# Row sums as a matrix product with ones stationary, rows divided before their turn, and key chunks taken three at a time in a BigBird attention kernel

## The chip, the core and the metric

The kernel runs on one core of one Trainium2 chip. Its time is the device time of one execution in microseconds (us), the median of three runs. Beside the runs there is one execution that was recorded by the hardware profiler; all durations below come from that one. TensorE is PE in the rows, its weight loads are PEld, VectorE is DVE, ScalarE is ACT, GpSimd is POOL, and SP is the queue from which most DMAs are issued.

## What is computed

Block-sparse attention over 4 batches, 8 heads, 768 positions and a head width of 64, and behind it a mixture of experts in which every token goes to one of 8 experts:

```python
scores = np.matmul(q, k.transpose(0, 1, 3, 2)) / np.sqrt(64)
scores = np.where(mask, scores, -1e9)          # window, first and last block, 3 sampled blocks a row
attn = np.exp(scores - scores.max(-1, keepdims=True))
attn = attn / (attn.sum(-1, keepdims=True) + 1e-09)
x = rows of np.matmul(attn, v)                 # (3072, 512): heads side by side
logits = x @ w_gate                            # (3072, 8); the largest chooses the expert
y = np.maximum(x[e's rows] @ w1[e], 0) @ w2[e] # 512 -> 1024 -> 512
out = softmax(logits)[chosen] * y
```

All of it is in 32-bit floats; the mask alone enters as bf16.

## The kernel before

**Attention.** The 32 heads are worked off as 16 pairs (4 batches by 4 pairs, number n in the code), each in two halves of 384 queries: 32 halves. Positions are spread so that a tile of 128 partitions holds six chunks of 128 keys. For each pair `load` (L88) brings k, q and v, and `turn` (L189) turns k and q on TensorE, so that the head width lies on partitions: three transposes into one PSUM bank, a copy of 384 columns to SBUF by VectorE, three more transposes into the same bank, and a copy by ScalarE. The k of the next pair is turned in the first half of this one, and its q in the second.

For each chunk of 128 keys `scores` (L208) does, for the two heads of the pair, the product of keys and queries (L216; the heads lie on partitions 0 to 63 and 64 to 127) and adds the mask as a second product (L219). ScalarE takes the exponential of both heads in one instruction (L221), and VectorE adds it up over the chunks into `esum` (L227), so that the sum over keys is left as a sum over partitions. `attend` (L229) multiplies with v: v's 64 columns of a head are stationary, the 384 columns of `e` move, and the two heads write partitions 0 to 63 and 64 to 127 of one bank `op` (L236). After the sixth chunk ScalarE copies `op` to `oT` (L241): outputs with the head width on partitions and queries along columns, not yet divided.

`rows_out` (L244) makes rows of them. First come the sums: for each of three query chunks and two heads a matmul in which 128 columns of `esum` are stationary and one column of ones moves (L252). Then three matmuls take `oT` as stationary and a matrix `mix` as moving operand (L257): `mix` is an identity with the gate's weights beside it, for each head apart, 144 columns, so that one product gives the turned rows and both heads' shares of the gate's logits. VectorE adds 1e-9 to the sums, takes their reciprocals (six columns), multiplies rows and logit shares by them while it copies them out of PSUM (L260 to L280), and SP stores the rows to `x_rows` in HBM. After the fourth pair of a batch `gate` takes the softmax over the experts.

**The order of work.** TensorE's and GpSimd's orders are those of the program text; VectorE's, ScalarE's and SP's come from a scheduler. The loop at L668 goes over steps of `GR = 2` chunks, three steps a half: it issues the scores of step i, and then the products with v of step i - 1. In the middle step of a half stand `turn` and, between its two sets of transposes, `rows_out` of the half before. PSUM has eight banks: two tiles of two banks for scores (`ps_s`), two banks for `op` (`ps_o`), one for turns (`ps_t`), one for `rows_out` and the routing (`ps_x`). Six `e` tiles are held.

**Routing.** When three of the four batches are done, `ranks`, `count`, `layout_a` and `tokens` (at pairs 12 to 14) work out on VectorE, with a few small matmuls, which tokens make the first 5 tiles of 128 rows of one expert each. So SP can load weights and GpSimd can gather rows before attention ends. The rest of the tokens are laid out in the same way behind it.

**Experts.** 28 such tiles follow, each with 4 MB of weights (two loads of 2 MB from SP), 32 matmuls in `layer1` (L622) and 8 wide ones in `layer2` (L642). `rows_out` of the very last half stands inside the first tile's `layer1`.

A matmul of 32-bit floats is one instruction in the program and two in the trace.

## Time and profile before

| | us |
|---|---|
| median of three runs | 846.18 (846.07 to 846.46) |
| the profiled execution | 846.65 |
| its span, first to last instruction | 844.9 |
| TensorE busy in the span | 820.4 |
| VectorE busy | 293.4 |
| ScalarE busy | 214.6 |
| GpSimd busy | 69.3 |
| attention, to the last product with v | about 421.9 |
| experts, from there | about 423.0 |

The first rows of the profile's page give busy time by engine. Busy time of TensorE says little by itself, because matmuls overlap and each is recorded from its start to its end: what one costs in a stream is the distance from its start to the start of the next. So the timeline is the view that prices TensorE's work here: it merges equal instructions that follow each other into one row and gives the start of each row to a hundredth of a microsecond. For VectorE and ScalarE the duration of an instruction is close to its price. "Granted clock" is the share of TensorE's full clock (2.4 GHz) that it was given in a stretch.

### The profile page before, as it was taken

Reading aid. Unit: us, or ns where it says so; the run is one execution under the profiler, and the core shown is the slowest. Engines: PE = TensorE matmul, PEld = TensorE weight load, DVE = VectorE, ACT = ScalarE, POOL = GpSimd, SP = SyncE. Lnnn points to the kernel's source line nnn. Section 1 sums busy time; section 2 is a strip of 40 time slices with the busy share of each in tenths; the row PEclk is TensorE's granted clock in tenths of the full one; section 3 lists DMA queues with packets and bytes.
Section 4 is the critical chain, followed back from the end, with each engine's and each line's share of the span. In section 5 each row is a group of like instructions: output and inputs, shape, how many; then the busy total and the mean of one; then the engine's idle time right before and its main releaser. Section 6 shows DMA issues by size and latency. Waiting matters only on the chain.

```text
span 844.9 us, 12494 instructions
## 1 busy us (share of the span) xinstructions
PE 820.4 (97%) x5104; PEld 519.8 (62%) x5104; DVE 293.4 (35%) x613; ACT 214.6 (25%) x306; POOL 69.3 (8%) x102
## 2 busy tenths in 40 slices
PE   7999999999999999899999999999999999999993
PEld 4555455455455455454587767686867777776681
DVE  5454565554554555854533001110101011111110
ACT  2444444544544544444411100000000000000000
POOL 4000000000000000002002111010101010111000
PEclk9999999999999999999999999999999999999997
DMA  7122221222321222842048989989899999999930
GB/s 168 41 74 57 75 67 47 60 73 57 76 70 44 62 71 58 277 178 70 20 164 299 331 326 325 334 304 337 305 335 309 336 312 336 325 332 340 324 127 10
DMA packets 119238, 157.52 MB, mean 186 GB/s; under 512 B 56435, under 2 KB 72819, under 8 KB 119156
## 3 DMA queue, kind: packets, MB, share of 16 engines
q1 hardware_dynamic: 112544, 142.32, 51.7%
q0 software_dynamic: 4480, 13.75, 4.2%
q8 instruction: 44, 0.72, 0.4%
q10 hardware_dynamic: 2132, 0.41, 0.2%
q14 instruction: 38, 0.31, 0.1%
HBM read 143.79 MB, written 13.73 MB: 186 GB/s over the span
## 4 chain that ended last, share of the span: by engine, by line
issue 44%; PE 42%; DMA 5%; POOL 4%; DVE 3%; another core or an unknown queue 0%; POOLq 0%; ACT 0%; DVEq 0%
PE s L216 15%; PE op L236 14%; DMA out_dram<-zo,sB 5%; PE xr L252 4%; PE s L219 3%; POOL xg L597 3%; PE xr L257 3%; PE tp L197 3%; POOL out_dram L654 1%; DVE esum L227 1%; PE first L197 0%; DVE allow L151 0%; DVE orA L561 0%; DVE kT L201 0%
## 5 line engine op out<-in xcount | busy, mean ns | idle before, releaser
L630 PEld LDWEIGHTS hp<-xgT,w 128*128 128x128 f32 x1792 | 206.3, 192 | 12.6 <-issue 12.6
L630 PE MATMUL hp<-xgT,w 128*128 128x128 f32 x1792 | 209.1, 275 | 0.0
L645 PE MATMUL zp<-w,hT 128*128 128x512 f32 x448 | 197.0, 593 | 0.9 <-DVE hT L635 0.9
L221 ACT ACTIVATE e<-s 128x768 f32<-128x768 f32 x192 | 155.6, 812 | 94.6 <-PE s L219 92.2
L216 PE MATMUL s<-qT,kT 64*128 64x384 f32 x768 | 167.4, 514 | 0.0
L227 DVE TENSOR_TENSOR esum<-esum,e 128x768 f32<-128x768 f32 x128 | 122.6, 958 | 69.5 <-ACT e L221 62.9
L236 PE MATMUL op<-e,v_sb 128*64 128x384 f32 x768 | 144.8, 499 | 0.0
L645 PEld LDWEIGHTS zp<-w,hT 128*128 128x128 f32 x448 | 83.1, 190 | 95.3 <-issue 94.2
L637 ACT ACTIVATE hT<-hp 128x512 f32<-128x512 f32 x33 | 19.7, 597 | 340.7 <-PE hp L630 337.8
L216 PEld LDWEIGHTS s<-qT,kT 64*128 64x128 f32 x768 | 64.0, 188 | 64.8 <-ACT e L221 37.4
L236 PEld LDWEIGHTS op<-e,v_sb 128*64 128x64 f32 x768 | 46.7, 136 | 80.1 <-issue 79.9
L653 DVE TENSOR_SCALAR zo<-zp,xg 128x512 f32<-128x512 f32 x23 | 17.3, 751 | 213.0 <-PE zp L645 194.0
L219 PE MATMUL s<-pen,oh 64*128 64x384 bf16 x384 | 63.6, 325 | 0.0
L227 DVE TENSOR_TENSOR esum<-e 128x768 f32<-128x768 f32 x32 | 30.7, 958 | 65.3 <-ACT e L221 65.3
L635 DVE TENSOR_SCALAR hT<-hp 128x512 f32<-128x512 f32 x23 | 15.9, 691 | 95.9 <-PE hp L630 95.9
L252 PEld LDWEIGHTS xr<-ones,esum 128*128 128x128 f32 x384 | 45.4, 192 | 1.2 <-DVE esum L227 1.2
L654 POOL DMA_INDIRECT out_dram<-zo,sB x23 | 23.3, 1014 | 269.6 <-DVE zo L653 269.6
L252 PE MATMUL xr<-ones,esum 128*128 128x1 f32 x384 | 44.9, 244 | 0.0
L219 PEld LDWEIGHTS <-oh 64*128 64x128 bf16 x384 | 19.5, 95 | 25.3 <-issue 0.9
L257 PE MATMUL xr<-mix,oT 128*128 128x144 f32 x192 | 31.4, 300 | 0.0
L597 POOL DMA_INDIRECT xg<-x_rows,gA x5 | 6.7, 1336 | 245.2 <-PE s L219 243.9
L257 PEld LDWEIGHTS xr<-mix,oT 128*128 128x128 f32 x192 | 25.4, 191 | 0.0
(185 smaller groups left out, 299.1 us busy)
## 6 DMA issues: line engine op xcount, KB each, us to landing
w<-in_moe_w_dram SPq DMA_DIRECT2D x56, 2048.0 KB, 9.7
k_sb<-in_k_dram SPq DMA_DIRECT2D x32, 192.0 KB, 3.4
v_sb<-in_v_dram SPq DMA_DIRECT2D x16, 384.0 KB, 3.1
x_rows<-xb SPq DMA_DIRECT2D x16, 384.0 KB, 3.8
q_sb<-in_q_dram SPq DMA_DIRECT2D x30, 192.0 KB, 3.2
q_sb<-in_q_dram ACTq DMA_DIRECT2D x2, 192.0 KB, 6.1
xg<-x_rows,gB POOLq DMA_INDIRECT x23, 7.7
out_dram<-zo,sB POOLq DMA_INDIRECT x23, 8.0
```

Source lines behind the costliest of these rows:

```text
L197: nc.tensor.transpose(tp[:, c * P : (c + 1) * P], src[:, half * HC + c].rearrange("p h d -> p (h d)"), ident[:],)
L216: nc.tensor.matmul(s[:, hh, :CW], lhsT=kT[r, c * P : (c + 1) * P], rhs=qT[r, cols], start=True, stop=False)
L219: nc.tensor.matmul(s[:, hh, :CW], lhsT=oh[r, c, :], rhs=pen[r, cols], start=False, stop=True)
L221: nc.scalar.activation(e[:], s[:, :, :CW], AF.Exp, scale=scale)
L227: nc.vector.tensor_add(t[:], es[(n, half, 0)][:] if c == 1 else t[:], e[:])
L236: nc.tensor.matmul(op[hh * D : (hh + 1) * D, :], lhsT=v_sb[:, hh, c, :], rhs=e[:, hh, :], start=(c == 0), stop=(c == NCH - 1),)
L252: nc.tensor.matmul(xr[:, HC * M + 2 * m + hh : HC * M + 2 * m + hh + 1], lhsT=esum[:, hh, m * P : (m + 1) * P], rhs=ones[:], start=True, s ...
L257: nc.tensor.matmul(xr[:, m * M : (m + 1) * M], lhsT=oT[:, m * P : (m + 1) * P], rhs=mix[:, pr, :], start=True, stop=True)
L597: nc.gpsimd.indirect_dma_start(out=xg[:], out_offset=None, in_=x_d[: N - S, :] if i < KA else x_d[:, :], in_offset=bass.IndirectOffsetOnAx ...
L630: nc.tensor.matmul(hp[:, m, :], lhsT=st[i]["w1"][:, c, fb * P : (fb + 1) * P], rhs=st[i]["xT"][:, c, :], start=(c == 0), stop=(c == DB - 1),)
L645: nc.tensor.matmul(zp[:], lhsT=st[i]["hT"][:, fb, :], rhs=st[i]["w2"][:, fb, :], start=(fb == 0), stop=(fb == FB - 1),)
L654: ins = nc.gpsimd.indirect_dma_start(out=out[:, :], out_offset=bass.IndirectOffsetOnAxis(ap=of("s", i, P), axis=0), in_=zo[:], in_offset=N ...
```

## The change

- `ones` becomes 64 columns wide. A new function `divide` runs once a half, straight behind the last products with v: the 64 columns of ones are stationary, `esum` moves (384 columns, for each head), and the two heads write partitions 0 to 63 and 64 to 127 of one bank `sp`. Every one of 64 partitions then holds the head's sums. ScalarE copies them to `ss` and adds 1e-9, SP stores one row a head into `sums` by a DMA from SBUF to SBUF, and VectorE takes reciprocals of `ss` in three instructions of 128 columns and multiplies `oT` with them.
- `rows_out` has no sums, reciprocals or multiplications left: three matmuls with `mix`, which needs only one set of gate columns now (136 columns), a copy of the rows and a copy or an addition of the logits, by VectorE. It runs for the pair before (n - 1), not for the half before. `oT` has four buffers.
- `GR` is 3: two steps a half. Eight `e` tiles are held.
- `turn` takes a `ps_s` tile (two banks): six transposes in a row, then two copies, both by ScalarE.
- PSUM: three tiles of two banks in `ps_s`, one bank for `op`, one in `ps_x`, which `divide` and `rows_out` share. `layer2` has its banks in a pool of its own.
- Routing of the first 5 tiles starts a half later, because rows come out later. At the end of attention `rows_out` of the last two halves stand in the middle of the first `layer1` and behind it.
- `judge`, a check of ranges that runs off the path in the second stage, reads the new shape of `sums`.

```diff
-    ps_t = ctx.enter_context(tc.tile_pool(name="ps_t", bufs=1, space=PSUM))
-    ps_o = ctx.enter_context(tc.tile_pool(name="ps_o", bufs=2, space=PSUM))
+    ps_o = ctx.enter_context(tc.tile_pool(name="ps_o", bufs=1, space=PSUM))
...
-    lend(lent, ps_s=2)
+    lend(lent, ps_s=3)
...
-    def turn(b, pr, which, first=None):
+    def turn(b, pr, which):
...
+        tp = upper["ps_s"].tile([P, 2, 512], F32, name="tp", tag="s")
+        for c in range(NCH):
+            nc.tensor.transpose(
+                tp[:, c // HC, c % HC * P : (c % HC + 1) * P], src[:, c].rearrange("p h d -> p (h d)"), ident[:],
+            )
         for half in range(2):
...
+            nc.scalar.copy(dst[:, half * CW : (half + 1) * CW], tp[:, half, :CW])
...
+    def divide(n, half):
+
+        oT, esum = ops_[(n, half)], esums.pop((n, half))
+        sp = ps_x.tile([P, CW], F32, name="sp", tag="xr")
+        for hh in range(2):
+            nc.tensor.matmul(sp[hh * D : (hh + 1) * D, :], lhsT=ones[:], rhs=esum[:, hh, :], start=True, stop=True)
+        ss = work.tile([P, CW], F32, name="ss")
+        nc.scalar.activation(ss[:], sp[:], AF.Copy, bias=1e-9)
+        row = 2 * (2 * n + half)
+        nc.sync.dma_start(sums[row : row + 2, :], ss.rearrange("(h d) q -> h d q", h=2)[:, 0, :])
+        r = work.tile([P, CW], F32, name="r")
+        for m in range(HC):
+            nc.vector.reciprocal(r[:, m * P : (m + 1) * P], ss[:, m * P : (m + 1) * P])
+        nc.vector.tensor_mul(oT[:], oT[:], r[:])
...
     def rows_out(n, half):
...
-        M = P + 2 * E
-        xr = ps_x.tile([P, HC * M + 2 * HC], F32, name="xr")
+        M = P + E
+        xr = ps_x.tile([P, HC, M], F32, name="xr")
         for m in range(HC):
-            for hh in range(2):
-                nc.tensor.matmul(
-                    xr[:, HC * M + 2 * m + hh : HC * M + 2 * m + hh + 1], lhsT=esum[:, hh, m * P : (m + 1) * P], rhs=ones[:],
-                    start=True, stop=True,
-                )
...
+            nc.tensor.matmul(xr[:, m, :], lhsT=oT[:, m * P : (m + 1) * P], rhs=mix[:, pr, :], start=True, stop=True)
...
+        nc.vector.tensor_copy(xb[:, half * HC : (half + 1) * HC, :], xr[:, :, :P])
...
+            nc.vector.tensor_copy(sofar, xr[:, :, P:])
         else:
...
+            nc.vector.tensor_add(sofar, sofar, xr[:, :, P:])
...
-    GR = 2
-    steps = [(n, half, g) for n in range(len(pairs)) for half in range(2) for g in range(NCH // GR)]
+    GR = NCH // 2
+    steps = [(n, half, g) for n in range(len(pairs)) for half in range(2) for g in range(2)]
...
                 attend(n, half, c)
+            if g == 1:
+                divide(n, half)
...
-            turning = turn(*pairs[n + 1], half) if n + 1 < len(pairs) else iter(())
-            next(turning, None)
-            if i > 3:
-                rows_out(*steps[i - 2][:2])
-            for _ in turning:
-                pass
-
-            if (n, half) == (NA, 0):
+            if n + 1 < len(pairs):
+                turn(*pairs[n + 1], half)
+            if n > 0:
+                rows_out(n - 1, half)
+
+            if (n, half) == (NA, 1):
                 ranks("A", 0, TA)
-            if (n, half) == (NA, 1):
+            if (n, half) == (NA + 1, 0):
                 count("A")
                 layout_a()
...
-    layer1(0, lambda: rows_out(*steps[-1][:2]), lambda: turn_x(1))
+    layer1(0, lambda: rows_out(len(pairs) - 1, 0), lambda: turn_x(1))
+    rows_out(len(pairs) - 1, 1)
```

What the diff does to the orders stands below at three places. In the rows of an order an instruction is named with its line, what it writes and reads, and the shape that it writes; a matmul of 32-bit floats is one instruction there.

TensorE before, at the middle step of a half (`op` the products with v, `tp` a turn, `xr` sums with ones and then rows with `mix`, `s` scores):

```order
L236 MATMUL op<-e,v_sb 64x384 x4
L197 MATMUL tp<-ident,q_sb 128x128 x3
L252 MATMUL xr<-ones,esum 128x1 x6
L257 MATMUL xr<-mix,oT 128x144 x3
L197 MATMUL tp<-ident,q_sb 128x128 x3
L216 MATMUL s<-qT,kT 128x384 x2
```

TensorE now, from the last scores of a half's first step (`sp` is the new sums):

```order
L215 MATMUL s<-pen,oh 128x384
L232 MATMUL op<-e,v_sb 64x384 x6
L245 MATMUL sp<-esum,ones 64x384 x2
L212 MATMUL s<-qT,kT 128x384 x2
L215 LDWEIGHTS oh
```

and from the last scores of its second step:

```order
L215 MATMUL s<-pen,oh 128x384
L232 MATMUL op<-e,v_sb 64x384 x6
L196 MATMUL tp<-ident,k_sb 128x128 x6
L262 MATMUL xr<-mix,oT 128x136 x3
L212 MATMUL s<-qT,kT 128x384 x2
```

Six matmuls that write one column each have given way to two that write 384, which follow products of their own shape; a half goes from scores to products with v twice, where it went three times.

VectorE before, over one half in the steady stretch:

```order
L227 TENSOR_TENSOR esum<-e 128x768
L227 TENSOR_TENSOR esum<-esum,e 128x768 x2
L201 COPY kT<-tp 128x384
L260 TENSOR_SCALAR sums<-xr 128x6
L261 RECIPROCAL r<-sums 128x6
L267 TENSOR_TENSOR xb<-xr,r 128x3x64 x2
L272 TENSOR_TENSOR lg<-xr,r 128x48
L279 TENSOR_TENSOR lgn<-lgn,lg 128x24
L280 TENSOR_TENSOR lgn<-lgn,lg 128x24
L227 TENSOR_TENSOR esum<-esum,e 128x768 x2
```

VectorE now:

```order
L223 TENSOR_TENSOR esum<-e 128x768
L223 TENSOR_TENSOR esum<-esum,e 128x768
L252 RECIPROCAL r<-ss 128x128 x3
L223 TENSOR_TENSOR esum<-esum,e 128x768
L253 TENSOR_TENSOR oT<-oT,r 128x384
L223 TENSOR_TENSOR esum<-esum,e 128x768 x2
L266 COPY xb<-xr 128x384
L271 TENSOR_TENSOR lgn<-lgn,xr 128x24
```

The turn's copy and the small instructions are gone; three reciprocals of 128 columns and a multiplication of 384 stand among the additions of `esum`.

SP now, where the first experts' weights are loaded (`xeA` the expert of a tile, `w_0` and `w_1` its weights):

```order
L249 DMA sums<-ss 2x384
L590 TENSOR_LOAD xeA
L590 ISA x2
L593 ISA
L593 DMA w_0_177<-in_moe_w_dram 128x4x1024
L249 DMA sums<-ss 2x384
L590 TENSOR_LOAD xeA
L590 ISA x2
L596 ISA
L596 DMA w_0_179<-in_moe_w_dram 128x8x512
```

The small stores of the sums, one a half, stand between these loads; before there was no such store.

## Rows read from the trace of the kernel before

**Rows 1.** The page, part 1: busy us and share of the span.
```profile
PE 820.4 (97%) x5104; PEld 519.8 (62%) x5104; DVE 293.4 (35%) x613; ACT 214.6 (25%) x306; POOL 69.3 (8%) x102
```

**Rows 2.** Busy time by stage, attention and experts; at the end granted clock, DMA share, GB/s.
```profile
0.00:421.90 421.90, 412.54 (x2711) 219.94 (x2711) 231.06 (x480) 188.23 (x261) 16.38 (x50) 1.00 0.31 82
421.90:844.90 423.00, 407.91 (x2396) 299.90 (x2394) 62.33 (x133) 26.36 (x45) 52.94 (x52) 0.99 0.82 290
```

**Rows 3.** Timeline of TensorE, one half: start us, us to the row's last end, work.
```profile
205.24 0.92 PE L216 MATMUL s<-qT,kT 64*128 64x384 f32 x4
205.99 0.33 PE L219 MATMUL s<-pen,oh 64*128 64x384 bf16 x2
206.15 0.81 PE L216 MATMUL s<-qT,kT 64*128 64x384 f32 x4
206.79 0.33 PE L219 MATMUL s<-pen,oh 64*128 64x384 bf16 x2
207.05 1.51 PE L236 MATMUL op<-e,v_sb 128*64 128x384 f32 x8
208.49 0.55 PE L197 MATMUL tp<-ident,q_sb 128*128 128x128 f32 x3
208.88 1.40 PE L252 MATMUL xr<-ones,esum 128*128 128x1 f32 x12
210.14 0.98 PE L257 MATMUL xr<-mix,oT 128*128 128x144 f32 x6
210.96 0.49 PE L197 MATMUL tp<-ident,q_sb 128*128 128x128 f32 x3
211.38 0.92 PE L216 MATMUL s<-qT,kT 64*128 64x384 f32 x4
...
221.15 0.55 PE L197 MATMUL tp<-ident,k_sb 128*128 128x128 f32 x3
```

**Rows 4.** Timeline of TensorE at the end of attention, two steps of products in a row.
```profile
419.15 2.80 PE L236 MATMUL op<-e,v_sb 128*64 128x384 f32 x16
421.88 3.84 PE L630 MATMUL hp<-xgT,w 128*128 128x128 f32 x32
```

**Rows 5.** VectorE by line and shape: busy us, mean ns, idle time before.
```profile
L227 DVE TENSOR_TENSOR esum<-esum,e 128x768 f32<-128x768 f32 x128 | 122.6, 958 | 69.5 <-ACT e L221 62.9
L201 DVE COPY qT<-tp 128x384 f32<-128x384 f32 x15 | 8.3, 551 | 0.0
L261 DVE RECIPROCAL r<-sums 128x6 f32<-128x6 f32 x32 | 6.1, 191 | 1.1
L260 DVE TENSOR_SCALAR sums<-xr 128x6 f32<-128x6 f32 x32 | 5.3, 164 | 50.8 <-PE xr L257 50.8
L298 DVE RECIPROCAL gs<-gs 128x6 f32<-128x6 f32 x4 | 0.7, 182 | 0.1
```

**Rows 6.** Timeline of VectorE: the narrowest instruction, one column.
```profile
441.36 0.13 DVE L523 TENSOR_SCALAR more_f<-upB 1x1 f32<-1x1 f32 x1
```

**Rows 7.** Busy time in a steady stretch and where routing begins (PE, PEld, DVE, ACT, POOL).
```profile
200.00:250.00 50.00, 50.00 (x334) 26.58 (x332) 27.13 (x55) 23.22 (x33) 0.00 (x0) 1.00 0.26 64
300.00:350.00 50.00, 48.98 (x326) 25.46 (x325) 33.73 (x93) 23.38 (x33) 0.00 (x0) 1.00 0.36 100
```

**Rows 8.** Waits of TensorE: us in total, times, longest.
```profile
PE tp L197 <- DVE kT L201: 2.0, 2, 1.3
PE first L197 <- DVE kT L201: 0.7, 1, 0.7
PE first L197 <- DVE qT L201: 0.7, 1, 0.7
```

**Rows 9.** Timeline of ScalarE: its copy of a turn.
```profile
211.48 0.48 ACT L203 COPY qT<-tp 128x384 f32<-128x384 f32 x1 [3.51 <-PE tp L197]
```

**Rows 10.** ScalarE by line: the exponentials, busy us, mean ns, idle time before.
```profile
L221 ACT ACTIVATE e<-s 128x768 f32<-128x768 f32 x192 | 155.6, 812 | 94.6 <-PE s L219 92.2
```

**Rows 11.** DMA issues: the weight loads, KB each, median us to landing.
```profile
w<-in_moe_w_dram SPq DMA_DIRECT2D x56, 2048.0 KB, 9.7
```

More of the change, by code (lines that the diff above doesn't have):

```diff
@@ L106 @@
     pen = mpool.tile([P, S], BF16, name="pen")
-    mix = mpool.tile([P, NPR, P + 2 * E], F32, name="mix")
-    ones = mpool.tile([P, 1], F32, name="ones")
-    sums = mpool.tile([P, 2 * B * NPR, HC, 2], F32, name="sums")
+    mix = mpool.tile([P, NPR, P + E], F32, name="mix")
+    ones = mpool.tile([P, D], F32, name="ones")
+    sums = mpool.tile([4 * B * NPR, CW], F32, name="sums")
     nc.vector.memset(ones[:], 1.0)
@@ L159, in make_mask @@
             nc.tensor.transpose(idle[:, 0, :P], ident[:], ident[:])
+        bm = upper["ps_s"].tile([P, 2, 512], F32, name="bm", tag="s")
         for half in range(2):
-            bm = ps_o.tile([P, HC, P], F32, name="bm", tag="o")
-            nc.tensor.matmul(bm[:], lhsT=allow2[:], rhs=oh[:NB, half * HC : (half + 1) * HC, :], start=True, stop=True)
+            nc.tensor.matmul(
+                bm[:, half, :CW], lhsT=allow2[:], rhs=oh[:NB, half * HC : (half + 1) * HC, :], start=True, stop=True,
+            )
+        for half in range(2):
             nc.vector.tensor_scalar(
-                pen[:, half * CW : (half + 1) * CW].rearrange("p (t q) -> p t q", t=HC), bm[:],
-                scalar1=-MASKED, scalar2=MASKED, op0=ALU.mult, op1=ALU.add,
+                pen[:, half * CW : (half + 1) * CW], bm[:, half, :CW], scalar1=-MASKED, scalar2=MASKED, op0=ALU.mult, op1=ALU.add,
             )
@@ L193, in turn @@
         turned.setdefault((b, pr), {})[which] = dst
[L194 to L204 removed]
+        tp = upper["ps_s"].tile([P, 2, 512], F32, name="tp", tag="s")
+        for c in range(NCH):
+            nc.tensor.transpose(
+                tp[:, c // HC, c % HC * P : (c % HC + 1) * P], src[:, c].rearrange("p h d -> p (h d)"), ident[:],
+            )
+        for half in range(2):
+            nc.scalar.copy(dst[:, half * CW : (half + 1) * CW], tp[:, half, :CW])
     es, ops_, esums, xbs, s_alls = {}, {}, {}, {}, {}
@@ L219, in scores @@
             nc.tensor.matmul(s[:, hh, :CW], lhsT=oh[r, c, :], rhs=pen[r, cols], start=False, stop=True)
-        e = work.tile([P, 2, CW], F32, name="e", bufs=6)
+        e = work.tile([P, 2, CW], F32, name="e", bufs=8)
         nc.scalar.activation(e[:], s[:, :, :CW], AF.Exp, scale=scale)
@@ L309, in shifted @@
         for c in range(NCH):
-            es[(n, half, c)] = work.tile([P, 2, CW], F32, name="e", bufs=6)
+            es[(n, half, c)] = work.tile([P, 2, CW], F32, name="e", bufs=8)
         for m in range(HC):
@@ L328, in shifted @@
                 for j in range(2):
-                    tp = ps_t.tile([P, CW], F32, name="tpq", tag="t")
+                    tp = upper["ps_t"].tile([P, CW], F32, name="tpq")
                     for c in range(HC):
@@ L343, in attention_again @@
             for which in range(2):
-                for _ in turn(*pairs[n], which):
-                    pass
+                turn(*pairs[n], which)
             for half in range(2):
@@ L611, in turn_x @@
     def turn_x(i):
-        tp = ps_t.tile([P, DB, P], F32, name="tp0", tag="t") if i == 0 else upper["ps_m"].tile([P, DB, P], F32, name="tpg")
+        if i == 0 and "ps_m" not in upper:
+            tp = upper["ps_s"].tile([P, 2, 512], F32, name="tp0", tag="s")[:, 0, :].rearrange("p (c q) -> p c q", c=DB)
+        else:
+            tp = upper["ps_m"].tile([P, DB, P], F32, name="tpg")[:]
         for c in range(DB):
@@ L642, in layer2 @@
     def layer2(i, group):
-        zp = ps_o.tile([P, DM], F32, name="zp", tag="o")
+        zp = upper["ps_z"].tile([P, DM], F32, name="zp")
         for fb in range(FB):
@@ L663 @@
     for which in range(2):
-        for _ in turn(0, 0, which, upper["ps_s"].tile([P, 2, 512], F32, name="first", tag="s")):
-            pass
-    GR = 2
-    steps = [(n, half, g) for n in range(len(pairs)) for half in range(2) for g in range(NCH // GR)]
+        turn(0, 0, which)
+    GR = NCH // 2
+    steps = [(n, half, g) for n in range(len(pairs)) for half in range(2) for g in range(2)]
     NA = (B - 1) * NPR
```

81 lines of the change are left out of this document (23 added, 58 removed).

## Prediction

> **What bounds the kernel now.** I read the busy times first: TensorE is busy 97% of the span, VectorE 35%, ScalarE 25% [rows 1]. By stage TensorE is busy 412.5 of 421.9 us in attention and 407.9 of 423.0 among the experts, and the granted clock is 1.00 and 0.99, the 2.4 GHz level, in both [rows 2]. The waits of TensorE name VectorE a few times, 3.4 us in the rows shown, and no DMA [rows 8]. So TensorE's stream is the path in both stages, the change touches the first alone, and what TensorE needs for one of the 32 halves is the number to work on. The timeline gives it: from one turn to the next 208.49 to 221.15, that is 12.66 us [rows 3].
>
> In that half three things are priced by distances between starts. Four passes of scores take 0.75 us when they follow products with v (205.24 to 205.99) and 0.64 when they follow scores (206.15 to 206.79); the mask's two take 0.16 when scores follow and 0.26 when products with v follow; eight passes of products with v take 1.44 (207.05 to 208.49) [rows 3]. Sixteen in a row take 2.73 (419.15 to 421.88) [rows 4], so eight more cost 1.29, four more 0.645, and a group of products pays 0.15 for beginning and ending. One visit of scores and back therefore costs 0.11 + 0.10 + 0.15, about 0.35 us, on top of the arithmetic. The sums with one moving column take 1.26 us (208.88 to 210.14): twelve passes of 0.105 although one column moves, while twelve weight loads of 128 columns stand behind them [rows 3].
>
> **The change, part by part.**
>
> *Sums.* The new sums are four passes of the shape and placing of the products with v and stand right behind them, so they lengthen that group: 0.645 us for 1.26. 32 x 0.615 = 19.7 us less. If the two heads' passes did not run side by side as those of v do, four passes would be 1.29 and nothing would be won here.
>
> *Three chunks a step.* Groups of scores fall from 96 to 64, so 32 visits of 0.35 go: 11.2 us less. The room for it is there: three `ps_s` tiles for three scores in a row, and three exponentials are 2.4 us [rows 10] in a half-step that has about 5.5. Bounds: 0, if another wait takes the place, and 11.2.
>
> *Rows with `mix`.* 136 columns for 144 in six passes that take 0.82 us now [rows 3]: at most 0.82 x 8/144 x 32 = 1.5 us less, nothing if the weight loads set the pace; I take 0.7.
>
> *Turns.* Twelve transposes' worth of TensorE time a pair is as before. The waits between a turn's first and second three (2.0 us in two places, and 1.4 in the first turn [rows 8]) go, since all six now have their own banks. Late next: scores of a new pair need the first copy of q, which ScalarE makes only once all six are done, 0.48 us [rows 9], and then a few hundredths on the way. Behind the turn stand the six passes of `rows_out`, about 0.8 us, which cover it with a tenth to spare. Where they are missing, before pair 1 and before the very first scores, about 0.6 us each is exposed. Net: 3.4 less, 1.2 more; 1.3 of the first belongs to routing, below. So 0.9 less here, and 0.4 more in case the tenth is missed now and then.
>
> *ScalarE.* One copy of `ss` and one more of a turn, 0.48 each [rows 9], on 23.2 busy of 50 [rows 7]: about 6.8 of 11.65 us a half. Its wait for the sums comes behind the copy of `op`, while TensorE is busy with three scores; the exponentials queued behind it start when those end. It costs nothing.
>
> *VectorE.* A half has five additions of 958 ns, and for the multiplication and the copy of rows, 384 columns each, I take the 551 of a copy of that width [rows 5], for the logits 0.2: 6.1 us, and three reciprocals r of 128 columns. The trace has none so wide. Below: it is like any instruction here, 164 ns for six columns and some 1.06 ns for each more, as between 384 and 768 columns: 0.29 us. Above: everything that six columns take beyond one column's 130 ns [rows 6] is by the column, (191 - 130) / 5 = 12 ns each: 1.68 us. Nearest lie the two reciprocals of six columns, which take 18 and 27 ns more than an addition to the same six [rows 5]: 3 to 4.5 ns a column beyond the 1.06, and so 0.7 to 0.9 us; I take 0.8. VectorE then needs 8.5 of 11.65 us a half, and even at 1.68 no more than 11.1. The additions for a half end some 3 to 4 us before its sums are called for, and rows, a pair late, have a whole half to spare. In steady halves it costs nothing.
>
> The place where it may cost is the routing of the first tiles, at pairs 12 and 13: VectorE has 6.6 us more work there in 50 (33.73 against 27.13 [rows 7]), nearly all in one half, and now the additions for the new sums queue behind it. 6.6 less the 3 free and the 3 to 4 of lead leaves 0 to 1; with what the ranks of the half before leave behind I take 2.8, against 1.3 that the turn waits there now: 1.5 more, between -1.3 at 0.29 and 8 at 1.68.
>
> What the Trainium skill says in VectorE: DVE Perf Modes, First, the fixed hardware budget speaks against the cheap reciprocal: it runs as an iterative divide with a repeat count of 8. At the 0.96 GHz of the skill's overview (Trainium Kernel Development and Optimization, NeuronCore Architecture) that is by estimate 1.07 us for 128 columns, with the fixed part 1.2, and the sum below would come out near 818. For six columns it would add 44 ns to an addition; the rows show 18 to 27 [rows 5], and no run here shows the wide one yet, so I stay with the rows.
>
> *SP.* The 32 small stores wait for `ss`, and behind them on SP stand the loads of k, q and v, issued a pair ahead, and the first weights. Weights come one between two stores, thus one about every half, and a load lands in 9.7 us [rows 11]. ScalarE writes `ss` again only two halves later, some 23 us, when the store has landed. Weights begin a half later than now and are still there before attention ends. Nothing.
>
> *The end.* The last two `rows_out` stand in and behind the first `layer1`; the last batch's routing then has the second `layer1`, over 7 us of TensorE, to hide in. Nothing. The experts' stage keeps its 423 us but for one set of sums, already counted.
>
> **The sum**, against the profiled execution's 846.65: -19.7 - 11.2 - 0.7 - 0.9 + 0.4 + 1.5 = -30.6, so 816.0; the median of the runs lies 0.5 lower, at 846.18, so **815.6 us**. A half is then 11.7 us. What a measurement of this kernel can tell from no change is about 0.2%, 1.7 us.
>
> **Rivals.**
>
> A. *Three chunks a step win nothing*: with all three `ps_s` tiles in one burst, or with one bank for `op` that must be copied before the next half's products, TensorE waits as long as the visits cost. For it: one bank less for `op`, and a turn takes a scores tile. Against: the copy of `op` has the sums and three scores, over 3 us, to be done in. 815.6 + 11.2 = 826.8.
>
> B. *The reciprocal lies near its upper end*, 1.4 to 1.7 us: steady halves still fit, but in routing VectorE falls some 8 us behind and TensorE waits for `esum` in front of the sums. 815.6 + 6.5 = 822. The skill's repeat count points this way, though by its estimate only to 1.2 us.
>
> C. *The change does not do what it says*: the passes of the two heads with ones run one after the other, 1.29 us for 1.26. For it: they were measured with v only. 815.6 + 19.7 = 835.3.
>
> D. *VectorE becomes the bound, and the kernel slower.* If the 191 ns for six columns are by the column, 32 ns each, 128 cost 4.1 us, and a half on VectorE 6.1 + 12.2 = 18.3 us for TensorE's 11.65: 32 x 6.65 = 213 us more, about 1028. It decides from 12.66 us a half, r = 2.2. Against: one column takes 130 ns, so most of the 191 is fixed.
>
> **Chances and range.** The forecast 0.68, with 810 to 820 as its own range (r at 0.29, `mix` at its full 1.5, up to a few microseconds more of waiting); A 0.12, B 0.12, C 0.04, D 0.02, and 0.02 for a wait that I do not see. 809 to 826 takes in the forecast, B and half of A, somewhat over 8 in 10. Faster by over 0.2%: 0.94, all but D, the unseen and a part of C; within 0.2%: 0.02; slower: 0.04.
>
> **What would show it.** Right: the timeline has sixteen passes in a row where the sums follow three chunks' products, 2.7 us to the next scores; turns of a steady stretch lie 11.7 us apart; the middle one of three scores takes 0.8 us; reciprocals of 128 columns take 0.7 to 0.9 us, and VectorE idles between additions. Wrong: turns over 12 us apart, the sums' row more than 0.7 us long beside the products (C), TensorE's waits naming `e` or `oT` (A), or naming `esum` in more halves than those of routing (B, D).

## The result: faster, by more than the range allowed

The changed kernel takes **808.34 us** (median of four runs, 806.37 to 809.33), the kernel before 846.12 beside it: a ratio of 0.9552, with a 95% interval from 0.9532 to 0.9573. The forecast was 815.6 and the range 809 to 826, so the sign was right and the gain, 37.8 us, was larger than the 30.6 forecast; the time lies 0.66 us below the range. Of the four runs one, 809.33, lies inside it. The profiled execution of after took 807.81 us, its span is 806.0, against 844.9.

The page, part 1, and the busy times by stage (columns as in [rows 2]; attention now ends at 383.9):

```profile
PE 784.2 (97%) x4850; PEld 490.6 (61%) x4850; DVE 342.3 (42%) x558; ACT 239.9 (30%) x370; POOL 67.5 (8%) x98
```
```profile
0.00:383.90 383.90, 376.42 (x2458) 191.25 (x2460) 276.36 (x423) 213.01 (x324) 14.53 (x46) 0.99 0.34 90
383.90:806.00 422.10, 407.80 (x2394) 299.31 (x2390) 65.91 (x135) 26.86 (x46) 52.94 (x52) 0.99 0.82 292
```

TensorE is busy for the same share as before [rows 1, 2] and has 36 us less to do in attention; VectorE has 49 us more in all and is still not the bound. The timeline of TensorE, one half from turn to turn (start, duration, work), answers to [rows 3]:

```profile
199.56 0.92 PE L212 MATMUL s<-qT,kT 64*128 64x384 f32 x4
200.31 0.33 PE L215 MATMUL s<-pen,oh 64*128 64x384 bf16 x2
200.47 0.81 PE L212 MATMUL s<-qT,kT 64*128 64x384 f32 x4
201.12 0.33 PE L215 MATMUL s<-pen,oh 64*128 64x384 bf16 x2
...
202.18 2.16 PE L232 MATMUL op<-e,v_sb 128*64 128x384 f32 x12
204.27 0.87 PE L196 MATMUL tp<-ident,k_sb 128*128 128x128 f32 x6
204.98 0.86 PE L262 MATMUL xr<-mix,oT 128*128 128x136 f32 x6
205.77 0.92 PE L212 MATMUL s<-qT,kT 64*128 64x384 f32 x4
...
208.39 2.16 PE L232 MATMUL op<-e,v_sb 128*64 128x384 f32 x12
210.38 0.81 PE L245 MATMUL sp<-esum,ones 128*64 128x384 f32 x4
211.12 0.92 PE L212 MATMUL s<-qT,kT 64*128 64x384 f32 x4
...
215.84 0.88 PE L196 MATMUL tp<-ident,q_sb 128*128 128x128 f32 x6
```

From turn to turn it is 11.57 us (204.27 to 215.84), where it was 12.66 and the prediction said 11.7. Products and sums together take 2.73 (208.39 to 211.12), just what sixteen passes in a row took in [rows 4], and scores follow scores at 0.81 to 0.91. VectorE by line and shape (busy us, mean ns, idle time before), and one half's reciprocals on its timeline, answer to [rows 5]:

```profile
L223 DVE TENSOR_TENSOR esum<-esum,e 128x768 f32<-128x768 f32 x128 | 120.5, 941 | 6.8
L252 DVE RECIPROCAL r<-ss 128x128 f32<-128x128 f32 x96 | 82.4, 914 | 36.5 <-ACT ss L247 35.3 <-ACT oT L237 1.2
```
```profile
200.20 2.58 DVE L252 RECIPROCAL r<-ss 128x128 f32<-128x128 f32 x3 [1.21 <-ACT ss L247]
```

A reciprocal of 128 columns is recorded with 914 ns; three of them take 2.58, so the next begins some 0.83 us after the one before. For VectorE the recorded duration is thus about a tenth above the price here, where it was taken as close to it ahead of the prediction. Busy times in the steady stretch answer to [rows 7]:

```profile
200.00:250.00 50.00, 50.00 (x332) 25.11 (x330) 37.29 (x55) 28.87 (x45) 0.00 (x0) 1.00 0.29 73
```

The waits of TensorE that the change leaves (in total, times, longest) answer to [rows 8]:

```profile
PE s L212 <- ACT qT L200: 1.1, 2, 0.6
PE tokA L557 <- DVE lgn L271: 1.0, 1, 1.0
PE cps L428 <- DVE lgn L269: 0.8, 1, 0.8
PE sp L245 <- DVE lgn L269: 0.4, 1, 0.4
```

None names `esum`, `e` or `oT`. The turn's wait for VectorE's copies is gone; one sums' wait of 0.4 has come in the routing. It names `lgn`, VectorE's last reading of the bank `ps_x`, which sums and rows share.

**Where 38.9 us of span went.** The copy of `op` to `oT` ends a half's products, so the distance from one to the next is the length of a half, with all that disturbs it.

| stretch | before | after | measured | predicted |
|---|---|---|---|---|
| to the first scores | 12.66 | 11.04 | -1.6 | -0.5 (turns) |
| first scores to the first `oT` | 15.55 | 14.55 | -1.0 | with the next |
| 31 distances between `oT`, as steady halves | 12.65 each | 11.57 each | -33.7 with remainders | -31.6 (sums, visits, `mix`, 32 halves) |
| what routing adds to its halves | 4.30 | 3.24 | -1.1 | +1.5 |
| last distance, beyond the steady difference | | | -0.7 | 0 |
| last `oT` to the end | 422.94 | 422.10 | -0.8 | 0 |
| sum | | | -38.9 | -30.6 |

Each column is one execution, and the start differs between executions of the same code. In e4, e6, e8, e9 and e10 (below), which do the same as the changed kernel up to the first `oT`, the first scores come at 10.40 to 11.44 and the first `oT` 14.89 to 15.68 later. So of the first two rows' 2.6 us the runs bear out between 1.1 and 2.5; the distances between `oT` in the steady stretch agree to 0.01 from half to half.

### The profile page after: what moved, and what is told of

Its sections match the earlier page's. It is cut to its first block, busy times and chain, and to the rows that moved or that the text cites. A ratio compares the mean times of both kernels' runs of the same rounds, so it can differ in the third digit from the quotient of the medians.

```text
span 806.0 us, 12186 instructions
## 1 busy us (share of the span) xinstructions
PE 784.2 (97%) x4850; PEld 490.6 (61%) x4850; DVE 342.3 (42%) x558; ACT 239.9 (30%) x370; POOL 67.5 (8%) x98
## 4 chain that ended last, share of the span: by engine, by line
issue 45%; PE 39%; DMA 6%; POOL 4%; DVE 3%; another core or an unknown queue 0%; POOLq 0%; ACT 0%; DVEq 0%
PE s L212 15%; PE op L232 14%; DMA xg<-x_rows,gB 6%; PE s L215 3%; PE tp L196 3%; POOL xg L584 3%; PE xr L262 2%; PE sp L245 2%; POOL out_dram L644 1%; DVE esum L223 1%; DVE r L252 0%; DVE allow L151 0%; DVE orA L548 0%; DVE xb L266 0%
## 5 line engine op out<-in xcount | busy, mean ns | idle before, releaser
L217 ACT ACTIVATE e<-s 128x768 f32<-128x768 f32 x192 | 152.9, 812 | 48.6 <-PE s L215 47.5
L212 PE MATMUL s<-qT,kT 64*128 64x384 f32 x768 | 163.4, 504 | 1.1 <-ACT qT L200 1.1
L232 PE MATMUL op<-e,v_sb 128*64 128x384 f32 x768 | 138.0, 494 | 0.0
L223 DVE TENSOR_TENSOR esum<-esum,e 128x768 f32<-128x768 f32 x128 | 120.5, 941 | 6.8
L212 PEld LDWEIGHTS s<-qT,kT 64*128 64x128 f32 x768 | 65.7, 188 | 53.2 <-issue 21.5
L252 DVE RECIPROCAL r<-ss 128x128 f32<-128x128 f32 x96 | 82.4, 914 | 36.5 <-ACT ss L247 35.3
L232 PEld LDWEIGHTS op<-e,v_sb 128*64 128x64 f32 x768 | 49.4, 136 | 76.0 <-issue 76.0
L223 DVE TENSOR_TENSOR esum<-e 128x768 f32<-128x768 f32 x32 | 30.6, 957 | 55.7 <-ACT e L217 55.7
L262 PE MATMUL xr<-mix,oT 128*128 128x136 f32 x192 | 27.7, 281 | 0.0
L237 ACT COPY oT<-op 128x384 f32<-128x384 f32 x32 | 15.3, 479 | 40.8 <-PE op L232 40.8
L245 PE MATMUL sp<-esum,ones 128*64 128x384 f32 x128 | 26.1, 487 | 0.4 <-DVE lgn L269 0.4
```

The costliest lines, as they stand in the source:

```text
L212: nc.tensor.matmul(s[:, hh, :CW], lhsT=kT[r, c * P : (c + 1) * P], rhs=qT[r, cols], start=True, stop=False)
L217: nc.scalar.activation(e[:], s[:, :, :CW], AF.Exp, scale=scale)
L223: nc.vector.tensor_add(t[:], es[(n, half, 0)][:] if c == 1 else t[:], e[:])
L232: nc.tensor.matmul(op[hh * D : (hh + 1) * D, :], lhsT=v_sb[:, hh, c, :], rhs=e[:, hh, :], start=(c == 0), stop=(c == NCH - 1),)
L245: nc.tensor.matmul(sp[hh * D : (hh + 1) * D, :], lhsT=ones[:], rhs=esum[:, hh, :], start=True, stop=True)
L252: nc.vector.reciprocal(r[:, m * P : (m + 1) * P], ss[:, m * P : (m + 1) * P])
```

## The experiments

The theory was the prediction's: TensorE's stream sets the time, and the old sums, the visits and the new sums each cost what their passes take. Each experiment changes one of these in the changed kernel. "The half" is the distance between two copies of `oT` in the steady stretch.

### The two kinds of sums

**e2_old_sums**: sums and division as before, all else as changed.

```diff
-            nc.tensor.matmul(sp[hh * D : (hh + 1) * D, :], lhsT=ones[:], rhs=esum[:, hh, :], start=True, stop=True)
...
+                nc.tensor.matmul(
+                    xr[:, HC * M + 2 * m + hh : HC * M + 2 * m + hh + 1], lhsT=esum[:, hh, m * P : (m + 1) * P], rhs=ones[:, :1],
+                    start=True, stop=True,
+                )
```

> The changed kernel with the sums as before: esum stationary, one column of ones moving, twelve passes in front of the rows, reciprocals of six columns and multiplications on VectorE behind them; three chunks a step, whole turns and the delay of rows by a pair stay as changed. As priced in the prediction (1.26 us for 0.645, 136 columns for 144) a half takes 11.57 + 0.62 + 0.04 = 12.23 us. If the one-column passes also delay the first pass with the mix matrix behind them (0.205 us to the next start, where the others have 0.12), a half takes 12.31. Kernel: 828 to 832 us.

834.57 us, ratio to the kernel before 0.9863 (0.9839 to 0.9886); the half is 12.30. So the old sums, with the 144 columns of `mix` that belong to them, cost 0.73 a half more than the new ones, where 0.615 and 0.02 were forecast. The half is the one expected for a delayed first pass with `mix`; the kernel lies above the 828 to 832 expected, mostly by one routing half (17.12 for 13.78 in the changed kernel) and by what follows the last `oT` (424.5 for 422.1).

**e9_no_sums**: the kernel leaves out both kinds.

```diff
-        for hh in range(2):
-            nc.tensor.matmul(sp[hh * D : (hh + 1) * D, :], lhsT=ones[:], rhs=esum[:, hh, :], start=True, stop=True)
...
-        nc.scalar.activation(ss[:], sp[:], AF.Copy, bias=1e-9)
+        nc.scalar.activation(ss[:], esum[:, 0, :], AF.Copy, bias=1.0)
```

> The changed kernel with the sums' matmuls left out: ScalarE copies the first head's partial sums, one key of each chunk to a partition, plus 1 in their place, so outputs are divided by the wrong numbers, tokens go to other experts, and only the halves of attention are read. It gives the bare half, against which both kinds of sums can be priced. If the new sums cost four more passes of products, 0.645 us, the half is 10.92 us. If the old sums cost the 1.26 us of their passes, their half of 12.30 would make it 11.04; if they also hold up the first pass with mix by 0.08, 10.96. Rival: beginning the sums behind the products has a price of its own, as beginning a group of scores has; then the half falls to about 10.8.

796.84 us in one run, with tokens at other experts, so that only the half counts: it is 10.92. New sums therefore cost 11.57 - 10.92 = 0.65, the 0.645 forecast for four more passes, and old ones, again with the 144 columns, 12.30 - 10.92 = 1.38, for which 1.26 had been read. The timeline of TensorE with the old sums shows where the 0.12 were:

```profile
201.99 1.40 PE L250 MATMUL xr<-ones,esum 128*128 128x1 f32 x12
203.25 0.98 PE L255 MATMUL xr<-mix,oT 128*128 128x144 f32 x6
204.16 0.92 PE L214 MATMUL s<-qT,kT 64*128 64x384 f32 x4
```

The sums take their 1.26, but the six passes with `mix` behind them take 0.91 to the next scores, where they take 0.79 in the changed kernel (204.98 to 205.77). Taken apart in the trace, the first of them is followed by the second after 0.205 us and the others after 0.1225, while in the changed kernel all six lie 0.116 to 0.118 apart: 0.08 (0.205 less 0.1225) is a delay behind the one-column passes, and the rest, 0.04, is that 144 columns are now 136 (0.1225 / 0.116 = 1.056, and 144 / 136 = 1.059, so columns set the pace). The delay stands in the trace of the kernel before in the same place with the same 0.205. What causes it was not tried.

**e10_sums_twice**: the new sums made twice.

```diff
-        for hh in range(2):
+        for hh in (0, 1, 0, 1):
```

> The changed kernel with the four passes of the new sums made twice, the second time over the first. If the two heads' passes run side by side as those with v do, a half takes 0.645 us more, 12.21 us, and the program 32 x 0.645 = 20.6 us more, 829 us. Rival (C of the prediction): one after the other, 1.29 more, 12.86 us a half, 849 us.

828.94 us in one run and a half of 12.21, that is 0.64 more. The two heads' passes run side by side; rival C falls.

### Three chunks a step

**e1_two_chunks**:

```diff
-    GR = NCH // 2
...
+    GR = 2
...
```

> The changed kernel with two chunks a step again (three steps a half, turn, sums and rows in the last one), all else as changed, three scores tiles included. Theory of visits: each of the 32 halves makes one visit from products with v to scores and back more, 0.35 us, so a half takes 11.57 + 0.35 = 11.92 us and the kernel 808.3 + 11 = 819.5 us. Rival A: the three-chunk step has won nothing, a half stays at 11.57 and the kernel within 2 us of 808.3.

821.55 us, ratio 0.9713 (0.9689 to 0.9737), 2 us above the 819.5 expected. The half is 11.92, so a visit costs 0.35 as read from [rows 3], and rival A falls. With old sums in their place as well, 11.57 + 0.35 + 0.73 = 12.65, the half of the kernel before: the two parts, measured one at a time, account for all of the steady gain.

**e11_two_score_tiles**:

```diff
-    lend(lent, ps_s=3)
+    lend(lent, ps_s=2)
```

> The changed kernel with two score tiles of two banks in place of three. If a third tile is what makes room for three scores in a row, the third score waits for the first exponential to end: it starts 0.92 + 0.16 behind the first score's end, and so some 0.3 to 0.4 us late in each of two steps a half, the turn waits for an exponential as well, and a half takes 12.2 to 12.6 us, 828 to 840 us in all, with waits of TensorE that name e. Rival: an exponential of 0.81 us keeps up with scores 0.80 apart, and two tiles do: 11.6 us, 808 us.

834.35 us in one run, a half of 12.36: without the third tile three chunks a step would lose more than they win. The timeline shows a third score that waits, and how little of that shows as idle time (the bracket):

```profile
190.18 0.33 PE L215 MATMUL s<-pen,oh 64*128 64x384 bf16 x2
190.66 0.92 PE L212 MATMUL s<-qT,kT 64*128 64x384 f32 x4 [0.15 <-ACT e L217]
191.41 0.33 PE L215 MATMUL s<-pen,oh 64*128 64x384 bf16 x2
```

From 190.18 to 190.66 are 0.48 us where 0.16 is usual, and the score itself then takes 0.75 to its mask in place of 0.65: the wait costs 0.42 and is shown with 0.15. In the other step of the half there is no bracket at all and the loss is 0.36.

### The turn in one piece

**e3_turn_split**: the turn in two sets of three transposes with the rows between them, as before, with the new tile and ScalarE's copies.

```diff
+            for c in range(half * HC, (half + 1) * HC):
+                nc.tensor.transpose(
+                    tp[:, c // HC, c % HC * P : (c % HC + 1) * P], src[:, c].rearrange("p h d -> p (h d)"), ident[:],
+                )
             nc.scalar.copy(dst[:, half * CW : (half + 1) * CW], tp[:, half, :CW])
+            yield
...
```

> The changed kernel with the turn cut in two again, three transposes on each side of the rows, into the same tile of two banks. If the 0.08 us a half by which the prediction fell short came from the old sums alone, a half stays at 11.57 to 11.60; if it came from the six transposes in a row, a half takes about 11.65.

813.3 us in one run; the half is 11.66, as expected if the six transposes in a row were what the prediction had missed. The trace gives the 0.09 another cause. TensorE's timeline in e3, then ScalarE's, and last VectorE's copy of a turn in the kernel before:

```profile
196.43 0.86 PE L263 MATMUL xr<-mix,oT 128*128 128x136 f32 x6
197.16 0.55 PE L197 MATMUL tp<-ident,q_sb 128*128 128x128 f32 x3
```
```profile
196.63 0.48 ACT L200 COPY qT<-tp 128x384 f32<-128x384 f32 x1 [1.74 <-PE tp L197]
```
```profile
209.13 0.55 DVE L201 COPY qT<-tp 128x384 f32<-128x384 f32 x1
```

The second three transposes go into the tile from which ScalarE copies the first three. They begin 0.05 us after that copy ends (196.63 + 0.48 = 197.11, and 197.16), and the same 0.05 stands in all 22 steady halves: they wait for the copy, though no idle time is shown in front of them. In the kernel before, the old sums stood between the two sets as well, and the second set began 1.27 us after the copy (209.69 to 210.96 [rows 3]). So e3 does not price a split as it was there. With old sums and the whole turn (e2) the half is the kernel before's less the visit alone: there the split cost nothing, and the whole turn is no third part of the steady gain. What the whole turn also changes is the start, told below.

### VectorE's room

**e4_reciprocals_twice**, and **e8_reciprocals_thrice** with three in place of two:

```diff
-        for m in range(HC):
+        for m in [m for m in range(HC) for _ in range(2)]:
             nc.vector.reciprocal(r[:, m * P : (m + 1) * P], ss[:, m * P : (m + 1) * P])
```

> The changed kernel with each reciprocal done twice (the second overwrites the first with the same values). VectorE needs 2.5 us more a half, some 11.1 of 11.57. If VectorE has its slack in steady halves, as forecast, these stay at 11.57 and only the routing halves grow, by 2 to 6 us in all: 810 to 815. If its additions are already what the sums wait for, every half grows: by up to 2.5 us, 840 to 890.

> Every reciprocal of 128 columns three times over. A half then asks of VectorE five additions x 0.96 + nine reciprocals x 0.83 to 0.91 + 0.55 + 0.55 + about 0.2 = 13.6 to 14.3 us, over the 11.57 us of TensorE's half, where twice over (11.1 to 11.6) it was still hidden. If VectorE is the other bound, a half takes 13.6 to 14.3 us and the program at least 32 x 2.0 = 65 us more: 870 to 910 us with the routing halves. Rival: the work runs beside TensorE whatever its amount and only the routing halves grow: 830 us.

Twice: 819.1 us, ratio 0.9679 (0.9647 to 0.9711). Steady halves stay at 11.57, and most of the loss is in routing, 16.76 and 18.42 where the changed kernel has 12.60 and 13.78, 8.8 us where 2 to 6 were expected (810 to 815 in all). Thrice: 869.65 us in one run, steady halves of 12.82, and the waits of TensorE now name VectorE all along. First the longest wait of twice, then that of thrice (in total, times, longest):

```profile
PE cps L428 <- DVE lgn L269: 4.4, 1, 4.4
```
```profile
PE sp L245 <- DVE lgn L271: 24.7, 21, 3.8
```

They name `lgn`, as in the changed kernel: a late VectorE holds TensorE up through the bank that it has not yet read out, and `esum` is named nowhere. Busy times of thrice from 200 to 250 us show the bound change hands (columns as in [rows 7]):

```profile
200.00:250.00 50.00, 45.85 (x297) 22.02 (x295) 49.52 (x73) 26.13 (x41) 0.00 (x0) 1.00 0.25 63
```

VectorE is busy 49.5 of 50 us here, TensorE 45.85. The mechanism of rival D is real; its point lies between two and three reciprocals of 0.83, 1.66 to 2.5 us a slice of 128 columns, and the change is at 0.83. The size was expected too high (13.6 to 14.3 a half) because durations were added, and the records of successive VectorE instructions overlap: three reciprocals recorded with 0.91 each take 2.58, and an addition recorded with 0.90 is followed after 0.81.

### The routing's halves

**e6_own_bank**: counts and token lists of the first routing phase in a score tile, not in the one `ps_x` tile that sums and rows share.

```diff
-        cps = ps_x.tile([P, 2, E], F32, name="cps", tag="xr")
+        cps = upper["ps_s"].tile([P, 2, 512], F32, name="cpsA", tag="s")[:, 0, : 2 * E].rearrange("p (a e) -> p a e", a=2) if own else ps_x.tile([P, 2, E], F32, name="cps", tag="xr")[:]
...
-        tp = ps_x.tile([P, 2, n], F32, name="tok" + ph, tag="xr")
+        tp = upper["ps_s"].tile([P, 2, 512], F32, name="tokS", tag="s")[:, 0, : 2 * n].rearrange("p (a e) -> p a e", a=2) if own else ps_x.tile([P, 2, n], F32, name="tok" + ph, tag="xr")[:]
...
```

> The changed kernel with the counts and the token lists of the first routing phase in score tiles in place of the one tile which sums and turned outputs share. If that shared tile is what TensorE waited for there (0.8, 1.0 and 0.4 us, named after the logits' add), these waits go and the program is 1.5 to 2.2 us faster than the changed kernel, about 806.3 us, the two routing halves at 11.8 to 12.5 us in place of 12.6 and 13.8. Rival: the matmuls wait for the routing's own VectorE chain, and the tile was only the last of two semaphores: within 0.5 us of the changed kernel, with the same halves.

806.8 us, ratio 0.9533 (0.9518 to 0.9549). The routing halves fall to 11.60 and 12.97, and the waits of 0.8 and 1.0 are gone (a wait of the sums of 0.8 us is what is left); the last `oT` comes 1.7 us earlier than in the changed kernel. So there the tile was waited for, not the routing's chain on VectorE. By the runs alone the two kernels' intervals overlap; the trace settles it.

### One step a half, and a version that beats both

**e5_six_chunks**, **e7_six_own_bank** (with the edit of e6) and **e12_six_gate_later** (also with the gate's exponential moved):

```diff
-    GR = NCH // 2
-    steps = [(n, half, g) for n in range(len(pairs)) for half in range(2) for g in range(2)]
+    GR = NCH
+    steps = [(n, half, g) for n in range(len(pairs)) for half in range(2) for g in range(1)]
...
```

All three also hold nine `e` tiles in place of eight, three `oT` and one `r`. And in e12 besides, where ScalarE's order, too, is that of the program text:

```diff
-    by_hand.enter_context(tc.manual_schedule(engines={mybir.EngineType.Pool, mybir.EngineType.PE}))
+    by_hand.enter_context(tc.manual_schedule(engines={mybir.EngineType.Pool, mybir.EngineType.PE, mybir.EngineType.Activation}))
...
-        nc.scalar.activation(ge[:], ge[:], AF.Exp)
+        def rest():
+            nc.scalar.activation(ge[:], ge[:], AF.Exp)
...
                 scores(n, half, c)
+            while late:
+                late.pop()()
```

> All six chunks of a half in one step: one visit of scores, then one of products and sums, where the changed kernel has two. If each visit costs the 0.35 us by which two chunks a step were slower than three (11.92 against 11.57 a half), a half falls to 11.22 us and the program by 32 x 0.35 = 11.2 us, to about 797 us. Rival: with three score tiles and six scores in a row, the exponentials (0.81 us each, against 0.80 us from one pass of scores to the next) set the pace, and the sums' tile, which the turned output needs next, comes free only after ScalarE has worked off six exponentials: a half stays at 11.5 to 11.6 us and the program at 806 to 809 us, with waits of TensorE for ScalarE's exponentials or for the sums' copy in the chain of waits.

> Both edits, six chunks a step and the routing's results in score tiles. If the two savings stand apart, the sum of them: about 11.2 + 1.8 us below the changed kernel, 795 to 796 us. Rival: with six scores in a row the score tiles are what is short, so that a score tile lent to the routing costs a score its place: no faster than six chunks alone, or slower by up to 1 us.

> Six chunks a step and the routing's results in score tiles, with the gate's exponential of 48 columns at the end of a batch put behind the six exponentials of the next half on ScalarE, where it now stands behind the first and waits there 1.2 us for VectorE's subtraction while five exponentials queue behind it. If that is what makes three halves at the batch ends 12.17 us in place of 11.27, they become 11.3 and the program 2.5 us faster than with six chunks and an own bank: about 802.3 us. Rival: something else in those halves (the reduction on VectorE before the logits are free, or the tile that sums and rows share) sets them, and they stay at 12.2: 804.8 us.

Six chunks alone win nothing: 808.72 us, 0.9556 (0.9539 to 0.9574). The steady half does fall, to 11.27 (0.05 short of the gain to 11.22: the first pass with `mix` is followed by the next after 0.172 in place of 0.118, perhaps because the bank that it shares with the sums has just been read, which was not tried). But three halves at the ends of batches take 12.17, the two routing halves 14.16 and 16.51 (waits of 2.7 and 3.0 for the shared tile), and the first `oT` comes 3.7 us later, as six scores now stand ahead of the first products; 2.1 of that comes back in the last half. ScalarE's timeline and then TensorE's show the end of a batch in e5:

```profile
213.71 0.81 ACT L217 ACTIVATE e<-s 128x768 f32<-128x768 f32 x1 [0.90 <-PE s L215]
215.73 0.24 ACT L285 ACTIVATE ge<-ge 128x48 f32<-128x48 f32 x1 [1.21 <-DVE ge L282]
```
```profile
215.12 0.81 PE L212 MATMUL s<-qT,kT 64*128 64x384 f32 x4
215.77 0.33 PE L215 MATMUL s<-pen,oh 64*128 64x384 bf16 x2
216.73 0.92 PE L212 MATMUL s<-qT,kT 64*128 64x384 f32 x4 [0.63 <-ACT e L217]
```

The gate's small exponential waits 1.21 us for VectorE, the large ones queue behind it, and scores find no free tile. With the routing's results in score tiles it is 804.77 us (e7, 0.9518, 0.9504 to 0.9531; one wait of scores of 1.6 us for the lent tile has come instead), and with that exponential behind the six large ones **801.01** (e12, 0.9471, 0.9458 to 0.9485): the three halves become 11.26 to 11.27, as expected, and the whole is 1.3 us below the 802.3 expected. As e12 fixes all of ScalarE's order, only these halves, and not the whole difference, show the exponential's part. The expectation of 795 to 796 for e7 had left out the fill and the batch ends.

## Why the prediction was right in its mechanism, and which of its steps failed

Two terms of the sum failed: the old sums, priced by their own row alone, were put too low, and the routing, put at 1.5 us more, came as 1.1 less. Each of them is larger than the 0.66 us by which the time left the range. The start and a rest add to the gain; all four errors have the same sign, so none hid another.

**Right.** TensorE's stream sets the time: it is busy for 50.00 of 50 us in the steady stretch. A visit costs 0.35 (measured 0.35), the new sums 0.645 (0.65), two heads side by side (e10). The reciprocal was taken at 0.8 us: recorded with 914 ns, 0.83 from one to the next. The Trainium skill's repeat count (VectorE: DVE Perf Modes, First, the fixed hardware budget) had given 1.2 by estimate; the trace does not agree with that. VectorE's load, 8.5 of 11.65 us, came out as 37.29 of 50 us in the steady stretch, or 8.6 of 11.57, and hides (e4). The exposed wait for q's copy comes in two places, shown with 1.1 us of idle time together, where 1.2 was forecast.

**Off: the sums' term (about 3 of 8.3 us).** The prediction charged the old sums "1.26 us (208.88 to 210.14)" [rows 3], the distance to the first pass with `mix`. With the columns of `mix` the runs give 1.38, and 0.73 for the exchange where 0.615 + 0.02 was forecast: the pass behind the first one with `mix` is 0.08 late, which lies in the next row, and the columns dropped from `mix` gave 0.04, not 0.02. Both stand inside the 0.82 that the prediction read for `mix`; what such a row takes without its neighbour could not be seen in the trace of before. Over 32 halves the 0.1 a half is the 3 us.

**Off: the routing (2.6 us).** "I take 2.8, against 1.3 that the turn waits there now: 1.5 more". The new wait in front of the sums is 0.38, and it is not for `esum`. TensorE's timeline of after and then of before, the rows with idle time, and last VectorE's of after ahead of the new wait:

```profile
322.35 0.17 PE L428 MATMUL cps<-endA,lt 128*128 128x8 bf16 x1 [0.84 <-DVE lgn L269]
339.20 0.87 PE L245 MATMUL sp<-esum,ones 128*64 128x384 f32 x4 [0.38 <-DVE lgn L269]
347.28 0.61 PE L557 MATMUL tokA<-tkA,orA 128*128 128x10 bf16 x18 [1.00 <-DVE lgn L271]
```
```profile
339.00 0.17 PE L441 MATMUL cps<-endA,lt 128*128 128x8 bf16 x1 [1.02 <-DVE lg L272]
352.84 0.55 PE L197 MATMUL tp<-ident,k_sb 128*128 128x128 f32 x3 [1.33 <-DVE kT L201]
379.62 0.61 PE L570 MATMUL tokA<-tkA,orA 128*128 128x10 bf16 x18 [0.93 <-DVE lg L272]
```
```profile
336.48 2.02 DVE L223 TENSOR_TENSOR esum<-esum,e 128x768 f32<-128x768 f32 x2
338.88 0.17 DVE L269 COPY lgn<-xr 128x24 f32<-128x24 f32 x1
```

The sum falls from 3.28 to 2.22, by as much as the routing's row in the table, 1.06. The last additions end at 338.50, before the products with v do at 338.8, so their lead was enough even here; the sums begin 0.15 after VectorE's copy of the logits, which frees the shared bank (339.05 to 339.20). The queue on VectorE that the prediction feared is there, but it reaches TensorE through that bank. e4 shows how near it is: with reciprocals of 1.66 the time is 819.1, in the direction of rival B and near its 822, though by waits for the bank, 4.4 us in front of the counts alone, and not for `esum`.

**Off: the start (1.1 us).** The prediction took the first turn's two waits at their idle time, 0.7 each [rows 8]. TensorE's timeline up to the first scores, before, after and in e4, whose start is the same code as after's:

```profile
7.33 0.82 PE L162 MATMUL bm<-oh,allow 24*128 24x384 bf16 x2 [2.64 <-DVE allow L155]
8.08 0.90 PE L197 MATMUL first<-ident,k_sb 128*128 128x128 f32 x3
9.63 0.90 PE L197 MATMUL first<-ident,k_sb 128*128 128x128 f32 x3 [0.65 <-DVE kT L201]
...
12.66 1.65 PE L216 MATMUL s<-qT,kT 64*128 64x384 f32 x4
```
```profile
7.31 0.49 PE L162 MATMUL bm<-oh,allow 24*128 24x384 bf16 x2 [2.67 <-DVE allow L155]
7.73 1.46 PE L196 MATMUL tp<-ident,k_sb 128*128 128x128 f32 x6
8.99 1.48 PE L196 MATMUL tp<-ident,q_sb 128*128 128x128 f32 x6
11.04 1.65 PE L212 MATMUL s<-qT,kT 64*128 64x384 f32 x4 [0.57 <-ACT qT L200]
```
```profile
7.29 0.81 PE L162 MATMUL bm<-oh,allow 24*128 24x384 bf16 x2 [2.60 <-DVE allow L155]
8.03 1.54 PE L196 MATMUL tp<-ident,k_sb 128*128 128x128 f32 x6
```

Six transposes without a wait are 1.26 from start to start (7.73 to 8.99), so three are 0.63; three and a wait of 0.65 were 1.55 (8.08 to 9.63). The wait cost 0.92. That the transposes also begin 0.35 earlier belongs to the execution and not to the change: the mask's two passes in front of them are recorded with 0.49 us in after and with 0.82 before, and in e4 they take 0.81 again and the transposes begin at 8.03. So some 0.75 of the 1.1 are the change's. With the turn split (e3) the first scores come at 12.47, and at 11.42 in e4.

**Not explained (1.5 us).** The last half is 0.7 better than its share and the experts' stage 0.8. Of the second, a wait of 0.9 us for `hT` in `layer2`, which before has and after has not, may be a part: the stage is 422.1 to 422.2 us long in after, e1 and e5 without it, and 422.5, 422.8 and 423.0 in e7, e11 and e12 with 0.3, 0.6 and 0.8 of it; but e10 has 422.6 without it. What decides it was not tried, and it is not shown to belong to the change.

The range's low end, 809, lay one below the forecast's own 810, which rested on r at 0.29 and `mix` at its full 1.5. It gave no room to sums that cost more than their own row, and none to routing that gets better with the reciprocal at 0.8; either would have held the result.

## What to carry to other kernels

A stream of matmuls is priced by starts, and the row behind a piece that goes belongs to its price: look for the same row elsewhere without that neighbour before calling it unchanged. An idle time in front of a TensorE row was less than what the wait cost in the three places priced here, and in one of them (e3) there was none to see; compare the start with the end of the copy that the row depends on. An experiment that gives the number expected can do so for another reason, as e3 did: look at what the edited piece waits for before reading its price. When one engine has room in the steady stretch, look for the stretch where it has not (routing here), and there ask which shared buffer the waits are for: a tile of its own bought back what the reciprocals were blamed for.

## What the runs showed of the hardware

- A wait in front of scores that is shown as 0.15 us of idle time cost 0.42, one of 0.65 in front of transposes 0.92, and one in front of e3's second transposes, shown with none, 0.09: the passes that follow a wait also take longer to their successor (0.75 for 0.65 in the first case).
- Twelve one-column passes take 0.105 us each, and behind them the first pass with `mix` is followed by the next after 0.205 in place of 0.1225 us: 0.08 of delay that stands in the next row.
- VectorE's successive records overlap by 0.08 us (0.914 recorded, 0.83 apart), so sums of durations put a full VectorE 0.8 to 1.5 us too high in 13 a half.
- At the start, scores take nearly twice as long as later, in both kernels (rows of 1.65 us at 12.66 before and at 11.04 after, 0.92 in the steady stretch). TensorE had done nothing from 4.7 to 7.3 us. After's record gives a granted clock of 0.50 from 11.04 to 14.40, the 1.2 GHz level. For before the view gives 1.00 from 12.66 to 16.02, with rows of the same durations; but the trace of before has no record of the clock ahead of 17.4 us, and the view counts a stretch without a record as full clock. So a 1.00 in the first microseconds can mean that nothing was recorded, and the durations have to be read beside it.
